# Ranking a gate's candidates by the softmax's sum, comparisons on ScalarE with TensorE counting, and one expert's activation placed earlier

## The chip, the cores and the metric

The kernel runs on one NeuronCore of a Trainium2 chip, in one launch. The metric is device microseconds of an execution, as the median of several runs. Five engines work side by side, each through its own list of instructions in order: TensorE (PE, its weight loads PEld), VectorE (DVE), ScalarE (ACT), GpSimd (POOL) and SyncE (SP), which here issues nearly all DMAs. SBUF and PSUM are the memories on the chip.

## The reference

The first half is a gated linear recurrence over 4 sequences of 5056 tokens with 256 channels; the second is a top-1 mixture of 8 experts with room for 80 tokens each.

```python
a_t = np.exp(8 * sigmoid(r_gate) * log_a_base)
x_gated = np.sqrt(np.maximum(1 - a_t * a_t, 1e-6)) * sigmoid(i_gate) * x
for t in range(S): h = a_t[:, t] * h + x_gated[:, t]; y[:, t] = h
# N = 20224 rows of y go to the experts
logits = x @ w_gate
expert_idx = np.argmax(logits, axis=1)
probs = np.exp(logits - logits.max(-1, keepdims=True))
probs /= probs.sum(-1, keepdims=True) + 1e-09
gate_w = probs[np.arange(N), expert_idx]
for e in range(8):
    # of the tokens whose argmax is e, the 80 with the largest gate_w
    h = np.maximum(x[tok_idx] @ w1[e], 0.0)
    out[tok_idx] = gate_w[tok_idx, None] * (h @ w2[e])
# every other row of out is zero
```

## The kernel before, in words

**Recurrence.** The tokens come in 40 blocks of 512 (`C`). A list written out by hand, `ORDER`, gives the order of all work of this half on every engine: loads, transposes on PE (L108, L142), tanh, exp and square root on ACT, products on POOL, the scan on DVE (L154). All states stay in SBUF, in the tile `Y`. Zeros go to the whole output from SP meanwhile (`zero_fill`, `wide_fill`).

**Gate.** PE forms logits from the states (L222). Six batches of blocks (`CHAINS`) go through eleven `stages`, which `ORDER` names c0.0 to c5.10: copy, transpose (L245), maximum, exp, the first expert at the maximum (`r_first`), the sum of the exps, then guard (L269), reciprocal (L271) and product (L274), a transpose back (`r_back`, L279) and a copy into `rows` (L283). After that each of 128 partitions of `rows` holds one expert's gate weights of a sixteenth of the tokens: partition 8j+e has expert e, share j. The token's weight stands in its own expert's row, zero in the other seven.

**Selection.** Written out in order in a block of its own, L391 to L451. Each partition takes its 14 largest weights (`K`): 8 with a maximum (L416), those replaced, the next 8 (L419). PE spreads the 14 of the 16 partitions that belong to one expert to all of them (L396), DVE scales them (`lowered`, L398). Then for each of the partition's own 14 a comparison with the expert's 224: `larger` compares on DVE (L401) and adds up on ACT (L402), for 12 of them (`SHARE`); `counted` does both on DVE (L404), for 2. The count is the candidate's rank. Between them stand, on POOL and DVE, the token numbers (L432 to L448) and the split of token and weight into parts in bf16 (`parts`, L410 to L413). PE runs twelve matmuls meanwhile whose result is not used (`keep_warm(WARM[0])`, L368), three before (`busy`, L101) and eight after. A comparison of the rank with 0 to 79 (L460) and 14 matmuls (L464) give each expert's 80 tokens and weights in order. A flag tells whether any partition had too few candidates; the arm for that does not run with these inputs.

**Experts.** Order by hand again (`experts`). For each expert the 80 tokens' columns are copied out of `Y`, split over ACT (`copies`, L544), POOL and DVE (L545) by the table `GATHER`, after each engine has loaded its token numbers into registers (`fetch`, L535). PE multiplies by w1 (`hidden`, L558), ACT applies the maximum with zero (`relu`, L563), PE multiplies by w2 (`summed`, L571), then a transpose (L586), the weight (`weigh`, L591) and a scatter into the output. Weights of two experts fit (`wbuf`): the loads of expert e+2 are issued from SP when `hidden(e)` and `summed(e)` are done with theirs (L322, L323), 512 KB each, four for an expert.

Of the kernel before, what the change touches and what calls it, by code (L numbers as in the profile page):

```python
# [19 lines left out]
SHARE = 12  # L20
WARM = (12, 8)
ZSLOT = 45
GATHER = ((28, 24), (28, 28), (32, 24))
# [36 lines left out]
def moe_kernel(ctx, tc, x, r_gate, i_gate, a_param, w_gate, w1, w2, out, capacity=80):  # L60
# [115 lines left out]
    nc.vector.tensor_tensor(fm, fm, bm, op=ALU.subtract)  # L176
# [12 lines left out]
    K1, NE = 16, P * EARLY  # L189
    rows = const.tile([P, NCOL + K1], F32, name="rows")  # L190
# [3 lines left out]
    for e in range(E): nc.gpsimd.memset(dio[:, e:e + 1], float(E - e))  # L194
# [102 lines left out]
    with tc.manual_schedule(engines={E_.Activation, E_.PE, E_.DVE, E_.Pool}):  # L297
        for task in ORDER.split():
            k, v = task[0], task[1:]
            if k in one_of: one_of[k](int(v))  # L300
            elif k in some_of: some_of[k](int(v.rstrip('+')), 1 + v.endswith('+'))
            elif k in half_of: half_of[k](int(v[:-1]), 'ab'.index(v[-1]))
            elif k == 'S': root(int(v.split(':')[0]), [int(m) for m in v.split(':')[1]])
            elif k == 'c': stages[int(v.split('.')[1])](int(v.split('.')[0]))
# [25 lines left out]
    V = 2 * E  # L330
    iot = lg[:, P:P + 80]
    se = lg[:, :P]
    nc.gpsimd.tensor_copy(se.rearrange("p (j e) -> p j e", e=E), em.unsqueeze(1).broadcast_to([P, NR, E]))
    nc.gpsimd.iota(iot, pattern=[[1, 80]], base=0, channel_multiplier=0, allow_small_or_imprecise_dtypes=True)
    small = lg[:, 208:512]
    comb = small[:, 210:210 + V]
# [45 lines left out]
    cmp = scr[:, 336:336 + 10 * 112].bitcast(BF16).rearrange("p (k j) -> p k j", k=10)  # L382
    oh = scr[:, 336:336 + K * CAP // 2].bitcast(BF16).rearrange("p (k s) -> p k s", s=CAP)
    vvf = scr[:, 1456:1712]; vv = vvf.rearrange("p (j k) -> p j k", j=NR)
    bd = scr[:, 1712:1968].rearrange("p (j k) -> p j k", j=NR)
    eq = scr[:, 1712:1968].rearrange("p (k q) -> p k q", k=16)
    late, tmp = rows[:, NE:], scr[:, 1200:1200 + K1 + NCOL - NE]
    pool, vec = nc.gpsimd, nc.vector
    pv = ps_t.tile([P, NR, 16], F32, name="pv")
    spare = bd  # L390
    with tc.manual_schedule(engines={E_.Activation, E_.PE, E_.DVE, E_.Pool}):  # L391
# [26 lines left out]
        vec.match_replace(tmp, cv[:, :8], late, -1.0)  # L418
        vec.max(cv[:, 8:], tmp)  # L419
        others_of(8, K)  # L420
        vec.max_index(ci[:, :8], cv[:, :8], late)
        lowered(0, 8); lowered(8, K)
        keep_warm(WARM[0], ps_t)
        parts(1, 3)
        larger(0)
        vec.max_index(ci[:, 8:], cv[:, 8:], tmp)
        pool.tensor_copy(pf, ci)
        larger(1)
# [3 lines left out]
        vec.tensor_tensor(eq, wide(pf), flat16(iot[:, :K1]), op=ALU.is_equal)  # L432
        pool.tensor_tensor(eq, eq, flat16(ecol), op=ALU.mult)
        larger(2); larger(3); larger(4)
        base(rk[:, :K], cv[:, :K], K)
        pool.tensor_scalar(lt, pf, float(K1), None, op0=ALU.is_ge)
        pool.tensor_scalar(cu.bitcast(F32), pf, float(NE - K1), None, op0=ALU.add)
        pool.tensor_tensor(lt, lt, cu.bitcast(F32), op=ALU.mult)
        vec.tensor_reduce(out=cf, in_=eq, op=ALU.add, axis=AX.X)
# [4 lines left out]
        for k in range(5, SHARE - 1): larger(k)  # L444
        vec.tensor_scalar(cu, cu, 5, None, op0=ALU.logical_shift_right)
        larger(SHARE - 1)
# [7 lines left out]
    nc.vector.tensor_scalar(fl, rk[:, K - 1:K], float(CAP), None, op0=ALU.is_lt)  # L454
# [12 lines left out]
    def general(K, ps):  # L467
# [9 lines left out]
        nc.vector.match_replace(rows[:, :NE], rows[:, NE + 8:NE + K1], rows[:, :NE], -1.0)  # L477
        bufs = (scr[:, :NCOL + K1], rows); cur = rows
        for r in range(K // 8):
# [3 lines left out]
            if r < K // 8 - 1:  # L483
                nc.vector.match_replace(bufs[r % 2], cv[:, sl], cur, -1.0)
# [12 lines left out]
        nc.vector.tensor_tensor(rk, rk, cnt, op=ALU.add)  # L497
# [13 lines left out]
    def experts(own, small_ps, ps, pool=True):  # L511
# [91 lines left out]
        def rows_of_slots():  # L603
# [5 lines left out]
            nc.vector.tensor_tensor(sidx, tk, none, op=ALU.add)  # L609
        small_ps.close()  # L610
# [75 lines left out]
```

## Time and profile before

| | us |
|---|---|
| median of 3 runs (294.41 to 295.31) | 294.52 |
| the profiled execution | 296.26 |
| its span, first to last instruction | 294.5 |
| busy: PE, DVE, ACT, POOL | 231.3, 212.6, 236.1, 209.4 |
| bytes moved by DMA, mean rate | 100.88 MB, 343 GB/s |

The span has three stretches: the recurrence up to about 214 us, the last gate batches and the selection up to 234, the experts up to the end. A time in the trace counts from the span's start. A row of the timeline has start, duration, engine, line, operation, tiles and shapes, a count where several were merged, and in brackets how long the engine had been idle and what ended that.

### The profile page before, as it was taken

The numbers are of one execution on the slowest core, as the hardware profiler recorded it, in microseconds if no ns is written. First come the engines' busy times: TensorE is split into PE (matmuls) and PEld (weight loads), VectorE is DVE, ScalarE is ACT, GpSimd is POOL, SyncE is SP. The second block draws the span as 40 slices with busy tenths as digits, with TensorE's granted clock in tenths as the row PEclk, the third lists the DMA queues.
The fourth block names the chain that finished last, engine by engine and source line by source line (L and its number), as shares of the span: only waits on it lengthen the run. The fifth ranks groups of instructions, "written<-read, shape, count | busy, mean of one in ns | idle before, by whom it ended". The sixth has DMA issues, their size and how long they took to land.

```text
span 294.5 us, 8439 instructions
## 1 busy us (share of the span) xinstructions
PE 231.3 (79%) x2816; PEld 189.6 (64%) x2816; DVE 212.6 (72%) x503; ACT 236.1 (80%) x480; POOL 209.4 (71%) x318
## 2 busy tenths in 40 slices
PE   2851796999988896897998888883786877999891
PEld 2750686777657764776765765852675667879780
DVE  2000596999989989999997999879968757566520
ACT  5899999999999999999999999599602457667600
POOL 2279999879959998998879964579204457775612
PEclk9965697999999999999999799799898999999997
DMA  6999799689999999999999999999999999999951
GB/s 216 417 410 410 273 415 411 240 320 416 410 406 337 347 375 352 359 365 325 374 352 368 333 340 323 335 312 325 406 395 409 355 379 343 328 358 356 319 159 31
DMA packets 42496, 100.88 MB, mean 343 GB/s; under 512 B 4048, under 2 KB 22352, under 8 KB 42448
## 3 DMA queue, kind: packets, MB, share of 16 engines
q1 hardware_dynamic: 42064, 99.64, 92.4%
q0 software_dynamic: 384, 0.66, 0.7%
q8 instruction: 24, 0.39, 0.5%
q14 instruction: 24, 0.20, 0.2%
HBM read 78.91 MB, written 21.36 MB: 341 GB/s over the span
## 4 chain that ended last, share of the span: by engine, by line
issue 11%; PE 11%; ACT 9%; DMA 9%; DVE 8%; POOL 6%; POOLq 2%; DVEq 1%; SPq 0%; ACTq 0%
DMA Y<-in_x_dram 5%; POOL Y L545 3%; ACT Y L119 3%; PE pd L368 2%; DVE Y L154 2%; DMA Y<-in_i_gate_dram 2%; PE pu L142 2%; ACT Y L131 2%; DMA Y<-in_moe_w_dram 2%; ACT Y L126 2%; POOLq L535 2%; ACT Y L110 2%; PE ph L558 2%; DVE pu L146 2%; PE pl L222 1%
## 5 line engine op out<-in xcount | busy, mean ns | idle before, releaser
L142 PE MATMUL pu<-ident,Y 128*128 128x128 f32 x632 | 91.5, 291 | 29.1 <-issue 10.4
L142 PEld LDWEIGHTS pu<-ident,Y 128*128 128x128 f32 x632 | 74.5, 149 | 48.4 <-issue 23.8
L154 DVE TENSOR_TENSOR_SCAN Y<-Y,pu 128x512 f32<-128x512 f32 (+4 forms) x86 | 100.6, 1179 | 2.7
L135 POOL TENSOR_TENSOR Y<-Y 128x1024 f32<-128x1024 f32 (+2 forms) x30 | 91.8, 3074 | 12.5 <-DMA Y<-in_x_dram 4.4
L122 POOL TENSOR_TENSOR Y<-Y 128x1024 f32<-128x1024 f32 (+2 forms) x30 | 72.8, 2438 | 24.1 <-ACT Y L119 11.8
L146 DVE SCALAR_TENSOR_TENSOR pu<-Y,pu 128x512 f32<-128x512 f32 (+1 forms) x80 | 53.6, 674 | 36.1 <-PE pu L142 32.5
L108 PE MATMUL pr<-ident,Y 128*128 128x128 f32 x316 | 46.6, 301 | 14.1 <-DMA Y<-in_r_gate_dram 8.1
L119 ACT ACTIVATE Y<-Y,tiny 128x512 f32<-128x512 f32 (+2 forms) x60 | 53.2, 945 | 0.3
L108 PEld LDWEIGHTS pr<-ident,Y 128*128 128x128 f32 x316 | 40.8, 157 | 16.6 <-ACT Y L110 10.2
L110 ACT ACTIVATE Y<-pr 128x1024 f32<-128x1024 f32 (+1 forms) x40 | 38.7, 1002 | 4.4 <-PE pr L108 4.4
L131 ACT ACTIVATE Y<-Y 128x1024 f32<-128x1024 f32 (+2 forms) x30 | 39.1, 1323 | 2.1 <-DMA Y<-in_i_gate_dram 1.5
L222 PE MATMUL pl<-Y 128*32 128x128 f32 (+2 forms) x704 | 40.4, 369 | 0.2 <-DVE Y L154 0.2
L126 ACT ACTIVATE Y<-Y 128x1024 f32<-128x1024 f32 (+2 forms) x30 | 37.9, 1319 | 0.1
L544 ACT COPY Y<-Y 128x2 f32 x248 | 24.7, 191 | 15.7 <-issue 10.6
L545 DVE COPY Y<-Y 128x2 f32 x196 | 22.3, 177 | 14.1 <-issue 14.1
L545 POOL COPY Y<-Y 128x2 f32 x196 | 24.8, 200 | 10.7 <-issue 10.7
L222 PEld LDWEIGHTS pl<-Y 128*32 128x32 f32 x704 | 19.9, 118 | 11.4 <-issue 5.0
L571 PE MATMUL po<-rows,Y 128*64 128x80 f32 x512 | 20.5, 235 | 3.8 <-ACT rows L563 2.2
L571 PEld LDWEIGHTS po<-rows,Y 128*64 128x64 f32 x512 | 18.7, 137 | 5.8 <-issue 2.7
L558 PE MATMUL ph<-Y 128*64 128x80 f32 x512 | 19.5, 234 | 2.9 <-DVE Y L545 2.1
L558 PEld LDWEIGHTS ph<-Y 128*64 128x64 f32 x512 | 18.5, 137 | 3.8 <-POOL Y L545 2.5
L126 ACT ACT_TABLE_LOAD x12 | 15.4, 1283 | 0.2
(137 smaller groups left out, 151.4 us busy)
## 6 DMA issues: line engine op xcount, KB each, us to landing
Y<-in_r_gate_dram SPq DMA_DIRECT2D x39, 512.0 KB, 7.2
Y<-in_i_gate_dram SPq DMA_DIRECT2D x39, 512.0 KB, 6.5
Y<-in_x_dram SPq DMA_DIRECT2D x39, 512.0 KB, 7.8
Y<-in_moe_w_dram SPq DMA_DIRECT2D x32, 512.0 KB, 6.0
out_dram<-Y SPq DMA_DIRECT2D x20, 512.0 KB, 6.7
out_dram<-Y SPq DMA_DIRECT2D x39, 256.0 KB, 7.0
Y<-in_r_gate_dram SPq DMA_DIRECT2D x1, 256.0 KB
Y<-in_i_gate_dram SPq DMA_DIRECT2D x1, 256.0 KB, 3.0
```

Source lines behind the costliest of these rows:

```text
L108: nc.tensor.transpose(pr[:, h, b:nb * P:nb], block('r', u, b, h), ident)
L110: nc.scalar.activation(rslot(u), prs.pop(u)[:, :, :ntok(u)], AF.Tanh, scale=0.5)
L119: nc.scalar.activation(a[:, :, h], z[:, :, h], AF.Exp, scale=L[:, h:h + 1], bias=L[:, h:h + 1])
L122: nc.gpsimd.tensor_tensor(pair('r', u, m), a, a, op=ALU.mult)
L126: nc.scalar.activation(q, q, AF.Sqrt, scale=-0.25, bias=0.25)
L131: nc.scalar.activation(i, i, AF.Tanh, scale=0.5)
L135: nc.gpsimd.tensor_tensor(i, i, v, op=ALU.mult)
L142: nc.tensor.matmul(pu[:, b:nb * P:nb], block(k, u, b, h), ident, is_transpose=True, start=(k == 'x' and b == 0), stop=(k == 'i' and b == n ...
L146: nc.vector.scalar_tensor_tensor(pu, rslot(u)[:, h], 0.5e-3, pu, op0=ALU.max, op1=ALU.mult)
L154: nc.vector.tensor_tensor_scan(y[:, s0:s1], a[:, s0:s1], q[:, s0:s1], init, op0=ALU.mult, op1=ALU.add)
L222: nc.tensor.matmul(pl[32 * j:32 * j + 32, c0:c0 + n], wg[:, h, 24 - E * k:WG - E * k], Y[:, us[0]:us[-1] + 1, h, 4 * j + k:ntok(us[0]):NR] ...
L545: else: eng.tensor_copy(dst, src)
```

## The change

**Value that is ranked.** The guard and the reciprocal of a batch go, and the product becomes a subtraction: in its own expert's row a token now holds minus the sum of its exps, in the others a number below -50. Weights 1/(sum + 1e-9) are formed for the chosen 80 at the end, two DVE instructions in `rows_of_slots`. Fill values become -1000.

**Comparisons.** Candidates are compared the other way round. Nine of the 14 on ACT: `Relu` with scale 2^40 and a bias for each partition, written as int8 into the low byte of bf16 numbers set to 128 before, so that a larger value adds 127. Five on DVE, written as bf16. The 14 results go to PE, which adds them over partitions and over candidates in one PSUM bank; DVE then keeps the partition's own part (a product, L470, and a sum, L471). No accumulator is read on ACT or DVE. Of the unused matmuls twelve become two; `busy` has four ahead of the transpose back and two more after each of the two spreads.

**Experts.** `relu(1)` moves ahead of ACT's last copies for expert 2, and `GATHER` gets an entry for each expert.

```diff
-SHARE = 12
-WARM = (12, 8)
+WARM = (2, 8)
-GATHER = ((28, 24), (28, 28), (32, 24))
+GATHER = ((28, 24), (28, 28), (28, 28), (28, 28), (28, 24), (32, 24), (28, 24), (32, 24))
...
-    nc.vector.tensor_tensor(fm, fm, bm, op=ALU.subtract)
+    nc.vector.scalar_tensor_tensor(fm, bm, 999.0, fm, op0=ALU.mult, op1=ALU.add)
...
-        d, key, top = view(pt, c), view(pt, c, 256), each(mx, c)
+        d, key, top = view(pt, c), view(lg, c, 256), each(mx, c)
         nc.vector.scalar_tensor_tensor(key, d, 0.0, dio[:d.shape[0]].unsqueeze(1).broadcast_to(list(d.shape)), op0=ALU.is_ge, op1=ALU.mult)
         nc.vector.tensor_reduce(out=top, in_=key, op=ALU.max, axis=AX.X)
-        nc.vector.tensor_tensor(view(lg, c, 256), key, spread(top), op=ALU.is_equal)
+        nc.vector.tensor_tensor(key, key, spread(top), op=ALU.subtract)
...
-    def r_guard(c):
-        by(c).tensor_scalar(each(sm, c), each(sm, c), 1e-9, None, op0=ALU.add)
-    def r_inverse(c):
-        nc.vector.reciprocal(each(sm, c), each(sm, c))
-    def r_weight(c):
+    def r_value(c):
         key = view(lg, c, 256)
-        by(c).tensor_tensor(key, key, spread(each(sm, c)), op=ALU.mult)
+        by(c).tensor_tensor(key, key, spread(each(sm, c)), op=ALU.subtract)
...
-        def larger(k):
-            c = cmp[:, k % 10]
-            vec.tensor_scalar(c.rearrange("p (j k) -> p j k", j=NR), vv[:, :, :K], cv[:, k:k + 1], None, op0=ALU.is_ge)
-            nc.scalar.activation(c, c, AF.Copy, accum_out=cnt[:, k:k + 1])
-        def counted(k):
-            vec.tensor_scalar(spare[:, :, :K], vv[:, :, :K], cv[:, k:k + 1], 0.0, op0=ALU.is_ge, op1=ALU.add, accum_out=cnt[:, k:k + 1])
+        def larger(q, k, act):
+            if act: nc.scalar.activation(low[q], vv[:, :, :K], AF.Relu, scale=BIG, bias=nb[:, k:k + 1])
+            else: vec.tensor_scalar(cmp[q].rearrange("p (j k) -> p j k", j=NR), vv[:, :, :K], cv[:, k:k + 1], None, op0=ALU.is_gt)
+        def summed(q, act, first, last):
+            nc.tensor.matmul(rps, seb[:, 0 if act else 1], cmp[q], start=first, stop=last)
+        nA = 9
+        def CA(k, first=False, last=False): larger(k % 4, k, True); summed(k % 4, True, first, last)
+        def CD(k): larger(4 + k % 3, nA + k, False); summed(4 + k % 3, False, False, False)
...
-        busy(3, ps_t.tile([P, 512], F32, name="pd"))
+        busy(4, bank)
...
+        vec.tensor_scalar(nb, cv, -BIG, None, op0=ALU.mult)
+        lowered(0, 8); lowered(8, K)
+        parts(1, 3)
+        CA(0, first=True); CA(1)
         vec.max_index(ci[:, :8], cv[:, :8], late)
-        lowered(0, 8); lowered(8, K)
-        keep_warm(WARM[0], ps_t)
...
         vec.tensor_scalar(cu, cu, 5, None, op0=ALU.logical_shift_right)
-        larger(SHARE - 1)
+        CA(8, last=True)
+        keep_warm(WARM[0], ps_t)
...
-        for k in range(SHARE, K): counted(k)
-        vec.tensor_tensor(rk[:, :K], rk[:, :K], cnt[:, :K], op=ALU.add)
+        vec.tensor_tensor(own[:, :, :K], rps.rearrange("p (j k) -> p j k", j=NR), bm.unsqueeze(2).broadcast_to([P, NR, K]), op=ALU.mult)
+        vec.tensor_reduce(out=red[:, :K], in_=own[:, :, :K].rearrange("p j k -> p k j"), op=ALU.add, axis=AX.X)
+        vec.tensor_tensor(rk[:, :K], rk[:, :K], red[:, :K], op=ALU.subtract)
...
-        for q in QS: first(q, 2); copies(q, 2)
+        for q in QS: first(q, 2)
+        copies('V', 2)
+        if pool: copies('P', 2)
+        copies('A', 2, 0, 20 if pool else 64)
         rows_of_slots()
         summed(0)
         hidden(1)
+        if pool: relu(1); copies('A', 2, 20)
         for k in range(1, E):
...
-            relu(k)
+            if k > 1 or not pool: relu(k)
```

On PE, from the warm-up ahead of the last transpose back (`pt`) to the flag's matmul (`pv` 1x1), before:

```order
L101 MATMUL pd<-ident 128x128 x3
L279 MATMUL pt<-ident,lg 128x112
L396 MATMUL pv<-Y,lg 128x16x8
L396 MATMUL pv<-Y,lg 128x16x6
L368 MATMUL pd<-Y,ident 128x256 x12
L456 MATMUL pv<-Y,lg 1x1
```

And the same place of the changed kernel; the pair at L412 is one comparison's weight load and matmul, and stands 14 times:

```order
L101 MATMUL pd<-ident 128x128 x4
L277 MATMUL pt<-ident,lg 128x112
L404 MATMUL pv<-Y,lg 128x16x8
L101 MATMUL pd<-ident 128x128 x2
L404 MATMUL pv<-Y,lg 128x16x6
L101 MATMUL pd<-ident 128x128 x2
L412 LDWEIGHTS Y
L412 MATMUL sel<-Y 128x224
...
L369 MATMUL pd<-Y,ident 128x256 x2
L477 MATMUL pv<-Y,lg 1x1
```

The transpose back now stands behind four unused matmuls, and fourteen counting matmuls have come in where ten unused ones went.

On DVE, the last part of the selection, from the sum that gives a token's column (`TENSOR_REDUCE` to `lg`) to the comparison with the 80 places, before:

```order
L439 TENSOR_REDUCE lg<-Y 128x16
L401 TENSOR_SCALAR Y<-Y,lg 128x224 x6
L445 TENSOR_SCALAR lg<-lg 128x16
L401 TENSOR_SCALAR Y<-Y,lg 128x224
L404 TENSOR_SCALAR Y,lg<-Y,lg 128x16x14 x2
L451 TENSOR_TENSOR lg<-lg 128x14
L454 TENSOR_SCALAR lg<-lg 128x1
L460 TENSOR_TENSOR Y<-lg 128x720
```

In the changed kernel:

```order
L458 TENSOR_REDUCE lg<-Y 128x16
L410 TENSOR_SCALAR Y<-Y,lg 128x224
L464 TENSOR_SCALAR lg<-lg 128x16
L470 TENSOR_TENSOR Y<-sel,Y 128x16x14
L471 TENSOR_REDUCE lg<-Y 128x14
L472 TENSOR_TENSOR lg<-lg 128x14
L475 TENSOR_SCALAR lg<-lg 128x1
L481 TENSOR_TENSOR Y<-lg 128x720
```

The shift of the token numbers (L445, now L464), for which POOL waits, has one comparison ahead of it instead of six, and two instructions on 224 numbers follow it.

On ACT, expert 1's activation (`rows<-ph`) among the copies for expert 2, from one load of token numbers to the next, before:

```order
L535 TENSOR_LOAD lg
L544 ISA
L544 COPY Y<-Y 128x2
...
L563 ACTIVATE rows<-ph 128x640
L581 COPY lg<-po 128x160
L535 TENSOR_LOAD lg
```

In the changed kernel, where the first stretch has 20 copies and the second 8:

```order
L556 TENSOR_LOAD lg
L565 ISA
L565 COPY Y<-Y 128x2
...
L584 ACTIVATE rows<-ph 128x640
L565 ISA
L565 COPY Y<-Y 128x2
...
L602 COPY lg<-po 128x160
L556 TENSOR_LOAD lg
```

The activation stood behind all 32 copies for expert 2 and now stands behind 20.

## Rows read from the trace of the kernel before

**Rows 1.** The page's DMA issues: tiles, engine, count, KB each, us to landing.

```profile
Y<-in_moe_w_dram SPq DMA_DIRECT2D x32, 512.0 KB, 6.0
```

**Rows 2.** Windows: us, busy of PE PEld DVE ACT POOL, granted PE clock, DMA share, GB/s.

```profile
226.00:228.00 2.00, 2.00 (x6) 1.64 (x5) 1.88 (x7) 1.35 (x7) 1.25 (x5) 0.50 1.00 395
...
246.00:249.00 3.00, 2.76 (x80) 2.60 (x76) 1.94 (x17) 1.94 (x20) 2.30 (x19) 1.00 0.95 309
...
252.00:255.00 3.00, 3.00 (x80) 2.72 (x78) 2.68 (x22) 2.56 (x28) 2.18 (x18) 1.00 0.84 283
...
270.00:280.00 10.00, 8.56 (x210) 7.69 (x211) 6.19 (x49) 6.92 (x61) 5.31 (x30) 1.00 0.94 317
```

**Rows 3.** Timeline, DVE and PE at the end of the last gate batch.

```profile
220.55 0.17 DVE L269 TENSOR_SCALAR Y<-Y 112x16 f32<-112x16 f32 x1
...
220.56 0.94 PE L101 MATMUL pd<-ident 128*128 128x128 f32 x6
...
220.76 0.25 DVE L271 RECIPROCAL Y<-Y 112x16 f32<-112x16 f32 x1
221.05 0.29 DVE L274 TENSOR_TENSOR lg<-lg,Y 112x128 f32<-112x128 f32 x1
...
221.40 0.32 PE L279 MATMUL pt<-ident,lg 112*128 112x112 f32 x1
```

**Rows 4.** Timeline, the selection from the scaled candidates to its last matmuls.

```profile
224.52 0.46 DVE L398 TENSOR_TENSOR Y<-pv,Y 128x128 f32<-128x128 f32 x2
...
225.12 7.11 PE L368 MATMUL pd<-Y,ident 128*128 128x256 f32 x24 [0.64 <-DVE Y L398]
...
228.46 1.59 DVE L401 TENSOR_SCALAR Y<-Y,lg 128x224 bf16<-128x224 f32 x6
...
230.30 0.28 POOL L447 TENSOR_SCALAR lg<-lg 128x16 f32<-128x16 int32 x1 [0.61 <-DVE lg L445]
...
230.78 0.45 DVE L404 TENSOR_SCALAR_CACHE_REDUCE Y<-Y,lg 128x224 f32<-128x224 f32 x1
...
231.22 0.38 POOL L411 TENSOR_TENSOR Y<-lg,Y 128x112 bf16<-128x112 bf16 x1
...
231.56 0.23 DVE L451 TENSOR_TENSOR lg<-lg 128x14 f32<-128x14 f32 x1 [0.33 <-ACT Y L402]
...
231.90 1.56 DVE L460 TENSOR_TENSOR Y<-lg 128x720 bf16<-128x720 f32 x2
...
232.11 0.92 POOL L411 TENSOR_TENSOR Y<-lg,Y 128x112 bf16<-128x112 bf16 x1
...
233.09 0.77 PE L464 MATMUL sel<-Y 128*48 128x80 bf16 x14 [0.74 <-POOL Y L411]
```

**Rows 5.** Lines of ACT, shapes apart: busy us, mean ns, idle before.

```profile
L119 ACT ACTIVATE Y<-Y,tiny 128x512 f32<-128x512 f32 x38 | 28.5, 809 | 0.1
...
L119 ACT ACTIVATE Y<-Y,tiny 128x1024 f32<-128x1024 f32 x20 | 23.7, 1238 | 0.2
...
L402 ACT ACTIVATE Y<-Y 128x224 bf16<-128x224 bf16 x12 | 4.5, 380 | 7.2 <-DVE Y L401 7.2
...
L402 ACT ACTIVATION_READ_ACCUMULATOR Y<-Y 128x1 f32 x12 | 2.2, 187 | 0.0
```

**Rows 6.** Timeline, PE and ACT from the start of the experts to expert 1's second product.

```profile
235.04 3.72 PE L368 MATMUL pd<-Y,ident 128*128 128x256 f32 x16
...
246.37 2.38 PE L558 MATMUL ph<-Y 128*64 128x80 f32 x64
...
246.94 3.35 ACT L544 COPY Y<-Y 128x2 f32 x32 [1.38 <-issue]
...
250.19 0.69 ACT L563 ACTIVATE rows<-ph 128x640 f32<-128x640 f32 x1
...
250.94 2.44 PE L571 MATMUL po<-rows,Y 128*64 128x80 f32 x64 [2.18 <-ACT rows L563]
```

**Rows 7.** Chain of waits, the piece behind expert 1's first product.

```profile
248.80 4.92 DMA Y<-in_moe_w_dram
```

More of the change, by code (lines that the diff above doesn't have):

```diff
@@ L9 @@
 I32 = mybir.dt.int32
+I8 = mybir.dt.int8
 U32 = mybir.dt.uint32
@@ L189, in moe_kernel @@
     K1, NE = 16, P * EARLY
+    LOW = -1000.0
     rows = const.tile([P, NCOL + K1], F32, name="rows")
@@ L193, in moe_kernel @@
     dio = tiny[:, 4:12]
-    for e in range(E): nc.gpsimd.memset(dio[:, e:e + 1], float(E - e))
+    for e in range(E): nc.gpsimd.memset(dio[:, e:e + 1], 100.0 * (E - e))
     lg = const.tile([P, C], F32, name="lg")
@@ L303, in moe_kernel @@
             elif k == 'S': root(int(v.split(':')[0]), [int(m) for m in v.split(':')[1]])
-            elif k == 'c': stages[int(v.split('.')[1])](int(v.split('.')[0]))
+            elif k == 'c':
+                if stages[int(v.split('.')[1])]: stages[int(v.split('.')[1])](int(v.split('.')[0]))
             elif k == 'Z': zero_fill(1)
@@ L330, in moe_kernel @@
     V = 2 * E
+    UNIT = 127
     iot = lg[:, P:P + 80]
@@ L333, in moe_kernel @@
     nc.gpsimd.tensor_copy(se.rearrange("p (j e) -> p j e", e=E), em.unsqueeze(1).broadcast_to([P, NR, E]))
-    nc.gpsimd.iota(iot, pattern=[[1, 80]], base=0, channel_multiplier=0, allow_small_or_imprecise_dtypes=True)
+    nc.gpsimd.iota(iot, pattern=[[UNIT, 80]], base=0, channel_multiplier=0, allow_small_or_imprecise_dtypes=True)
     small = lg[:, 208:512]
-    comb = small[:, 210:210 + V]
+    comb = small[:, 210:210 + V]; i16 = small[:, 226:242]
+    nc.gpsimd.iota(i16, pattern=[[1, K1]], base=0, channel_multiplier=0, allow_small_or_imprecise_dtypes=True)
     nc.vector.tensor_tensor(comb[:3 * V], ident[:3 * V, :V], ident[:3 * V, V:2 * V], op=ALU.add)
@@ L381, in moe_kernel @@
     rr = scr[:, :K * 3 * V // 2].bitcast(BF16).rearrange("p (k q v e) -> p k q v e", k=K, q=3, v=2)
-    cmp = scr[:, 336:336 + 10 * 112].bitcast(BF16).rearrange("p (k j) -> p k j", k=10)
+    KJ = NR * K
+    cmp = [scr[:, 336 + KJ // 2 * q:336 + KJ // 2 * (q + 1)].bitcast(BF16) for q in range(7)]
+    low = [scr[:, 336 + KJ // 2 * q:336 + KJ // 2 * (q + 1)].bitcast(I8).rearrange("p (j k b) -> p j k b", j=NR, b=2)[:, :, :, 0] for q in range(4)]
+    seb = scr[:, 1120:1248].bitcast(BF16).rearrange("p (q m) -> p q m", q=2)
     oh = scr[:, 336:336 + K * CAP // 2].bitcast(BF16).rearrange("p (k s) -> p k s", s=CAP)
[L384 to L387, printed above, removed]
+    tmp = scr[:, 1248:1248 + K1 + NCOL - NE]
+    vvf = scr[:, 1504:1760]; vv = vvf.rearrange("p (j k) -> p j k", j=NR)
+    bd = scr[:, 1760:2016].rearrange("p (j k) -> p j k", j=NR)
+    eq = scr[:, 1760:2016].rearrange("p (k q) -> p k q", k=16)
+    own = scr[:, 1760:2016].rearrange("p (j k) -> p j k", j=NR)
+    late = rows[:, NE:]
+    nb, red = small[:, 112:128], small[:, 242:258]
+    BIG = 2.0 ** 40
     pool, vec = nc.gpsimd, nc.vector
     pv = ps_t.tile([P, NR, 16], F32, name="pv")
-    spare = bd
+    rps = ps_t.tile([P, 512], F32, name="sel")[:, :KJ]
     with tc.manual_schedule(engines={E_.Activation, E_.PE, E_.DVE, E_.Pool}):
@@ L414, in moe_kernel @@
         pool.memset(rr[:, :, 2, 0], 0.0)
-        busy(3, ps_t.tile([P, 512], F32, name="pd"))
+        pool.tensor_copy(seb[:, 0], se)
+        pool.tensor_scalar(seb[:, 1], se, float(UNIT), None, op0=ALU.mult)
+        for q in range(4): pool.memset(cmp[q], 128.0)
+        bank = ps_t.tile([P, 512], F32, name="pd")
+        busy(4, bank)
         vec.max(cv[:, :8], late)
         others_of(0, 8)
-        vec.match_replace(tmp, cv[:, :8], late, -1.0)
+        busy(2, bank)
+        vec.match_replace(tmp, cv[:, :8], late, LOW)
         vec.max(cv[:, 8:], tmp)
         others_of(8, K)
+        busy(2, bank)
+        vec.tensor_scalar(nb, cv, -BIG, None, op0=ALU.mult)
+        lowered(0, 8); lowered(8, K)
+        parts(1, 3)
+        CA(0, first=True); CA(1)
         vec.max_index(ci[:, :8], cv[:, :8], late)
-        lowered(0, 8); lowered(8, K)
-        keep_warm(WARM[0], ps_t)
-        parts(1, 3)
-        larger(0)
         vec.max_index(ci[:, 8:], cv[:, 8:], tmp)
         pool.tensor_copy(pf, ci)
-        larger(1)
+        CA(2); CD(0); CA(3); CD(1)
         wide = lambda v: v.unsqueeze(2).broadcast_to([P, 16, K1])
         flat16 = lambda v: v.unsqueeze(1).broadcast_to([P, 16, K1])
[L432 to L435, printed above, removed]
+        vec.tensor_tensor(eq, wide(pf), flat16(i16), op=ALU.is_equal)
         pool.tensor_scalar(lt, pf, float(K1), None, op0=ALU.is_ge)
@@ L438, in moe_kernel @@
         pool.tensor_tensor(lt, lt, cu.bitcast(F32), op=ALU.mult)
+        pool.tensor_tensor(eq, eq, flat16(ecol), op=ALU.mult)
+        CA(4); CD(2)
+        base(rk[:, :K], cv[:, :K], K)
+        vec.tensor_scalar(rk[:, :K], rk[:, :K], float(UNIT * (KJ - K) + 128 * NR * nA), None, op0=ALU.add)
+        CA(5); CD(3); CA(6)
         vec.tensor_reduce(out=cf, in_=eq, op=ALU.add, axis=AX.X)
@@ L443, in moe_kernel @@
         pool.tensor_scalar(vals[:, 0], cf, float(NR), m1, op0=ALU.mult, op1=ALU.add)
-        for k in range(5, SHARE - 1): larger(k)
+        CA(7); CD(4)
         vec.tensor_scalar(cu, cu, 5, None, op0=ALU.logical_shift_right)
-        larger(SHARE - 1)
+        CA(8, last=True)
+        keep_warm(WARM[0], ps_t)
         pool.tensor_scalar(cf, cu, float(C), None, op0=ALU.mult)
@@ L476, in general @@
         eq = scr[:, :K * K1].rearrange("p (k q) -> p k q", q=K1)
-        nc.vector.match_replace(rows[:, :NE], rows[:, NE + 8:NE + K1], rows[:, :NE], -1.0)
+        nc.vector.match_replace(rows[:, :NE], rows[:, NE + 8:NE + K1], rows[:, :NE], LOW)
         bufs = (scr[:, :NCOL + K1], rows); cur = rows
@@ L483, in general @@
             if r < K // 8 - 1:
-                nc.vector.match_replace(bufs[r % 2], cv[:, sl], cur, -1.0)
+                nc.vector.match_replace(bufs[r % 2], cv[:, sl], cur, LOW)
                 cur = bufs[r % 2]
@@ L609, in rows_of_slots @@
             nc.vector.tensor_tensor(sidx, tk, none, op=ALU.add)
+            nc.vector.tensor_scalar(AT[:, E:], AT[:, E:], -1.0, 1e-9, op0=ALU.mult, op1=ALU.add)
+            nc.vector.reciprocal(AT[:, E:], AT[:, E:])
         small_ps.close()
```

14 lines of the change are left out of this document (7 added, 7 removed).

## The prediction

> **What bounds the kernel now.** I read the windows first, stretch by stretch, then the timeline from the last gate batch to the first experts, then the chain of waits, and the lines of ACT for the price of one comparison. The change touches nothing that the long recurrence waits for, so the last 75 us of the span count, and they have two parts.
>
> The first, from about 220 to 240 us, is one chain without slack: transpose back, candidates, comparisons, ranks, places, token numbers, gather. The reader sees in it that each step starts where another engine ends: POOL's token arithmetic waits 0.61 us for one shift on DVE, DVE's first use of the ranks waits 0.33 us for ACT, and the 14 matmuls that place the tokens wait 0.74 us for POOL's split of the token numbers [rows 4]. So at the end of the selection POOL is last, not ACT, although ACT's adding up is what the change replaces.
>
> The second, the experts, is held by PE and by the stream of weights together. There are 32 loads of 512 KB [rows 1], and the DMA share is 0.95 to 0.84 in two windows around expert 1 and 0.94 near the end [rows 2]; the rest of the time the engines are full. PE has one large hole: after expert 1's first product, which ends at 248.75 us, it waits 2.18 us for the activation, and ACT reaches this at 250.19 only, behind 32 copies for expert 2 [rows 6]. The chain of waits names a weight load there [rows 7].
>
> **The change part by part.** *Start of the selection.* Guard and reciprocal of the last batch go: from the start of L269 to the start of L274 DVE spends 0.50 us, so the value is ready at 220.84 instead of 221.34. But PE has four warm-up matmuls ahead of the transpose now. Six passes (three matmuls) took 0.94 us from 220.56, 0.157 each; eight take 1.25, and the transpose, which started 0.09 us ahead of the six passes' end, starts at 221.72 instead of 221.40 [rows 3]. The 0.50 us is lost and 0.3 us more: the selection starts 0.3 us late. If the passes follow each other closer, it is 0.1 us; below nothing it cannot be, since PE keeps its order. In the earlier batches the same instructions go from DVE at a time when the DMA engines are the limit; I count nothing, and nothing is lost if that cover goes.
>
> *DVE in the selection.* Twelve comparisons become five: seven at 1.59/6 = 0.265 us, 1.86 us. Two compare-and-count go, 0.48 us from one start to the next, 0.96 us. The wait for ACT, 0.33 us, goes [rows 4]. New are two small ones on 16 numbers (as L269, 0.17 us each [rows 3]) and two on 224 (as L404, 0.45 us each [rows 4]): 1.24 us. Net 1.9 us less; with the late start the ranks are ready 1.6 us sooner, at 230.2 instead of 231.79, if nobody makes DVE wait.
>
> *ACT in the selection.* Twelve ACTIVATEs of 0.380 us with twelve reads of 0.187 become nine ACTIVATEs. No row shows this form (f32 in, every second byte out, a bias by partition). From below, the same 224 numbers take 0.380 us [rows 5]. From above, L119 has scale and bias by partition: 0.809 us for 512 and 1.238 for 1024, so 0.84 ns a number and 0.38 us fixed, 0.57 us for 224 [rows 5]. Nine take 3.4 or 5.1 us; from 225.1 us they end at 228.5 or 230.2, the last counting matmul some 0.3 us later, and three DVE instructions (about 1.1 us) follow. At the lower end DVE is later anyway, at the upper one only 0.2 us of the selection is won. I take 0.40, nearest to the row with the same shape, and keep both ends.
>
> The Trainium skill, ScalarE: Activation LUTs, "What ACT_TABLE_LOAD costs", gives 186 ns and 0.833 ns an element for an ACTIVATE, 93 ns more for each per-partition operand, and 93 ns of overlap between two in a row; by it nine of these end after 3.45 us (an estimate), and the sum stays as it is. The trace agrees where it can: the formula gives 0.80 us for L119 on 512 numbers, the row has 0.809.
>
> *POOL.* The shift that it waits for stands behind one comparison instead of six; the 0.61 us goes. Its three small operations now run while DVE forms the 256-number comparison, ahead of the product instead of behind it, which is worth up to 0.5 us more. Against it, both numberings of candidates now end 0.2 us later than before, since they stand behind the scaling. Between 0.4 and 1.3 us sooner; I take 1.0. The last split took 0.92 us beside DVE's L460 where it took 0.38 without [rows 4]; it will meet that again, so nothing is won there. The placing matmuls start when POOL is done, at 232.1 instead of 233.09. **Selection: 1.0 us sooner**, range 0.2 to 1.5. The new casts and fills on POOL come while it waits for the last batch.
>
> *Experts.* Shifted by 1.0, ACT's copies for expert 2 start at 245.94. Twenty take 20 x 3.35/32 = 2.09 us, to 248.03, past the end of the product at 247.75; the activation's 0.69 us ends at 248.72, and the second product starts at about 248.8 instead of 250.94 [rows 6]: 2.1 us sooner, 1.1 of it from the move. The eight copies behind the activation and the fetch for expert 3 are late next: they push expert 3's gather, which limits what arrives to about 1.9 us. Four copies that ACT loses in three experts go to POOL or DVE, which have as many already; I count nothing, or 0.4 us either way if the balance shifts. The two new instructions for the weights stand where DVE waits for expert 2.
>
> The sum is 1.9 us. The profiled execution took 296.26 us, with a span of 294.5, so it would take 294.4; the median of the runs is 1.7 us below the profiled one, so the same difference gives 294.52 - 1.9 = **292.6 us**.
>
> **The rivals.** *The weights decide.* By the DMA shares the stream left about 3 x 0.05 + 3 x 0.16 = 0.6 us unused around expert 1 and 10 x 0.06 = 0.6 near the end [rows 2]. If loads of 512 KB that take 6.0 us to land [rows 1] cannot start earlier in step with PE, only part of the first 0.6 is gained: 0.4 us, 294.1 us. For it speaks the chain's DMA piece of 4.92 us [rows 7]; against it, that the second product of expert 1 was itself late and issues the loads of expert 3.
>
> *The selection gains nothing.* The late transpose, slow ACTIVATEs or POOL's split eat the 1.0; the move of the activation alone gives 1.1: 293.4 us. For it speak the upper price of ACT and the four warm-ups; against it, the three waits that vanish.
>
> *The clock.* Slower than before. PE stood mostly idle ahead of 225 us and was granted 0.50 in 226 to 228, the lower of 1.2 and 2.4 GHz [rows 2]; 24 passes took 7.11 us [rows 4], where 16 at the higher level took 3.72 [rows 6], so 24 would take 5.58: one drop cost 1.5 us of PE time. It was paid by matmuls that nobody waits for; ten of these twelve are gone, and the counting matmuls are short. One drop in the placing matmuls costs tenths. If two such drops reach the expert products, which have no slack, it is 3.0 us: 294.52 - 1.9 + 3.0 = 295.6 us. The second one decides. Against it stand the eight warm-ups ahead of expert 0, which remain.
>
> The Trainium skill, TensorE: Matmul & The Clock Gate, Part 1, says that the gate passes half the pulses by default and all of them when the array has been busy. By it this rival is open in principle; the row above agrees.
>
> **How the numbers follow.** Forecast 0.60 (291.3 to 293.5), selection without gain 0.15 (293.4), weights 0.15 (294.1), clock and other losses 0.10 (about 295.6). What this measurement can tell from no change is about 0.3%, 0.88 us: faster means under 293.6, slower over 295.4. The first two cases are faster, 0.75; the third is the same, 0.15; slower 0.10. The upper end of the range takes in the third case and half of the last, 295.2; the lower, 291.1, is a selection 1.5 us sooner and both 0.6 us of the stream filled with something to spare. Outside are about 0.06 on either side.
>
> **What would show it.** Transposing back at or after 221.6 us; nine ACTIVATEs within 3.4 to 4 us; the first DVE use of the counts without a wait for ACT; the placing matmuls at about 232, released by POOL; expert 1's second product within 0.2 us of the activation, near 248.8; the DMA share between 252 and 255 close to 1. I am wrong if ACT's comparisons last 5 us, if PE's clock is 0.50 in the first expert products, or if PE's holes behind expert 2 grow by what expert 1 saved.

## The result, and the profile after

The changed kernel takes 298.7 us (median of 4 runs, 297.9 to 300.3) against 294.47 of the kernel before (4 runs, 293.12 to 295.31): ratio 1.0147 [1.0102, 1.0191], **slower by about 4.3 us**. The prediction was 292.6, faster.

The profiled execution of before lay 1.8 us over its median, that of after 0.8 below its own, so the two traces differ by 1.4 us of span only (294.49 and 295.86). They still show the places. Against before, the last scan of the recurrence ends 2.04 us later (217.49, 215.45). From there to the placing matmuls it is 0.15 longer, from those to expert 1's second product 1.53 shorter, from that to expert 4's first product 3.25 longer, and from there to the end 2.54 shorter. The sum is 1.37. In that last stretch PE's products by w2 for experts 4 and 5 took 2.43 to 2.44 us, where before they took 2.76 to 2.81 and the one for expert 6 was broken by 1.20 us; that the loads of weights had run ahead during the longer wait is likely, but not shown.

**Recurrence.** First the view of one line, the third instruction of `r_first` (duration in ns: least, median, most), which had its `key` in PSUM before:

```profile
L264 DVE TENSOR_TENSOR lg<-pt,Y x6: 291/424/424, 84.5 to 220.0; 128x256 f32<-128x256 f32 x4, 128x128 f32<-128x128 f32 x1, 112x128 f32<-112x128 f32 x1
```

and after, where `key` stands in SBUF:

```profile
L265 DVE TENSOR_TENSOR lg<-lg,Y x6: 292/787/3267, 85.8 to 222.1; 128x256 f32<-128x256 f32 x4, 128x128 f32<-128x128 f32 x1, 112x128 f32<-112x128 f32 x1
```

The same instruction on the same 256 numbers now takes up to 3.27 us. The timeline of DVE and POOL around the longest one:

```profile
158.77 3.60 POOL L122 TENSOR_TENSOR Y<-Y 128x2048 f32<-128x2048 f32 x1
...
159.38 3.27 DVE L265 TENSOR_TENSOR lg<-lg,Y 128x256 f32<-128x256 f32 x1
...
162.33 4.71 POOL L135 TENSOR_TENSOR Y<-Y 128x2048 f32<-128x2048 f32 x1
162.57 0.68 DVE L146 SCALAR_TENSOR_TENSOR pu<-Y,pu 128x512 f32<-128x512 f32 x1
```

It started while a product of POOL ran, and ended 0.28 us after that product's end (162.37 to 162.65). The same batch of before, beside the same POOL product:

```profile
157.29 3.61 POOL L122 TENSOR_TENSOR Y<-Y 128x2048 f32<-128x2048 f32 x1
...
158.21 0.42 DVE L264 TENSOR_TENSOR lg<-pt,Y 128x256 f32<-128x256 f32 x1
160.55 1.29 DVE L146 SCALAR_TENSOR_TENSOR pu<-Y,pu 128x512 f32<-128x512 f32 x2 [1.91 <-ACT Y L126]
```

Here DVE is done in 0.42 us and then waits 1.91 for ACT: part of the 3.27 us falls into a wait that was there, the rest delays the scans. The Trainium skill, SBUF — State Buffer, "Who interferes with whom", states it as a rule: a DVE instruction with both inputs in SBUF contends with a GpSimd instruction that reads SBUF, and what they contend for, a shared pair of ports, is an exclusive lock. The trace agrees in three of six instances (1.15, 3.27 and 1.21 us); of the other three, two had no POOL product beside them, and one started 0.13 us before a product ended and took 0.42.

The 2.04 us by which the last scan ended later cannot be read as the price of this: in the traces with `key` in PSUM that scan ended anywhere from 213.72 (b3) to 216.99 us (c3).

**Selection.** The timeline that answers to [rows 3, 4]:

```profile
222.66 0.29 DVE L272 TENSOR_TENSOR lg<-lg,Y 112x128 f32<-112x128 f32 x1
...
223.03 1.16 PE L101 MATMUL pd<-ident 128*128 128x128 f32 x8
...
224.02 0.26 PE L277 MATMUL pt<-ident,lg 112*128 112x112 f32 x1
...
227.64 3.46 ACT L409 ACTIVATE Y<-Y,lg 128x224 int8<-128x224 f32 x9 [6.18 <-DVE Y L406]
...
229.99 0.80 DVE L410 TENSOR_SCALAR Y<-Y,lg 128x224 bf16<-128x224 f32 x1
230.00 0.65 POOL L453 TENSOR_TENSOR Y<-Y,tiny 128x256 f32<-128x256 f32 x1
...
231.73 0.17 DVE L464 TENSOR_SCALAR lg<-lg 128x16 int32<-128x16 int32 x1 [0.38 <-POOL lg L461]
...
232.80 0.21 DVE L472 TENSOR_TENSOR lg<-lg 128x14 f32<-128x14 f32 x1
...
233.12 1.58 DVE L481 TENSOR_TENSOR Y<-lg 128x720 bf16<-128x720 f32 x2
...
233.40 0.89 POOL L424 TENSOR_TENSOR lg<-lg 128x16 f32<-128x16 f32 x1
...
234.85 0.38 POOL L422 TENSOR_TENSOR Y<-lg,Y 128x112 bf16<-128x112 bf16 x1
...
235.28 0.68 PE L485 MATMUL sel<-Y 128*48 128x80 bf16 x14 [1.83 <-POOL Y L422]
```

The value is ready at 222.95 and its transpose starts at 224.02, behind the unused matmuls; before, the two stood 0.06 apart (221.34, 221.40). From the transpose on, the ranks (L472) come after 8.99 us where they came after 10.39, so DVE and ACT gave 1.4. The placing matmuls come after 11.26 us where it was 11.69: they wait 1.83 us for POOL's split, 0.74 before. DVE waits for POOL now (0.38), where POOL waited for DVE.

**Experts.** PE and POOL from expert 1's second product to expert 4's first one, in the timeline that answers to [rows 6]:

```profile
251.60 2.43 PE L592 MATMUL po<-rows,Y 128*64 128x80 f32 x64 [0.80 <-ACT rows L584]
...
257.76 2.44 PE L579 MATMUL ph<-Y 128*64 128x80 f32 x64 [1.02 <-POOL Y L566]
...
266.18 2.43 PE L579 MATMUL ph<-Y 128*64 128x80 f32 x64 [3.27 <-POOL Y L566]
```

and POOL's own rows:

```profile
253.93 3.67 POOL L566 COPY Y<-Y 128x2 f32 x28 [1.37 <-issue]
261.59 1.13 POOL L615 DMA_INDIRECT out_dram<-Y,lg  x1 [3.99 <-DMA Y<-in_moe_w_dram]
263.11 3.02 POOL L566 COPY Y<-Y 128x2 f32 x24 [0.39 <-issue]
```

The hole behind expert 1's first product has shrunk from 2.18 to 0.80 us. A new one of 3.27 has come ahead of expert 4's first product: the copies for expert 4 stand behind the first scatter in POOL's order, and POOL idles 3.99 us ahead of that scatter. The row that the scatter sends was ready at 256.41 and the copies ended at 257.60. The releaser named, a load of weights, is nothing that the scatter needs. Before, the scatter started at 254.83, 0.82 us behind the copies:

```profile
250.99 3.02 POOL L545 COPY Y<-Y 128x2 f32 x24 [1.24 <-issue]
254.83 1.14 POOL L594 DMA_INDIRECT out_dram<-Y,lg  x1 [0.82 <-DVE Y L545]
256.33 0.79 POOL L545 COPY Y<-Y 128x2 f32 x6 [0.37 <-issue]
257.30 2.27 POOL L545 COPY Y<-Y 128x2 f32 x18 [0.17 <-issue]
```

The last two rows are the copies for expert 4, which come behind that scatter; the break of 0.17 us between them is taken up below, under c3.

### The profile page after: what moved, and what is told of

The parts are those of the page before. It is cut to its first block, busy times and chain, and to the rows that moved or that the text cites. A ratio compares the mean times of both kernels' runs of the same rounds, so it can differ in the third digit from the quotient of the medians.

```text
span 295.9 us, 8429 instructions
## 1 busy us (share of the span) xinstructions
PE 226.3 (76%) x2820; PEld 184.9 (62%) x2820; DVE 214.6 (73%) x498; ACT 233.6 (79%) x449; POOL 212.0 (72%) x329
## 5 line engine op out<-in xcount | busy, mean ns | idle before, releaser
L108 PE MATMUL pr<-ident,Y 128*128 128x128 f32 x316 | 43.2, 284 | 17.0 <-DMA Y<-in_r_gate_dram 8.8
L108 PEld LDWEIGHTS pr<-ident,Y 128*128 128x128 f32 x316 | 36.8, 147 | 20.5 <-ACT Y L110 11.7
L565 ACT COPY Y<-Y 128x2 f32 x232 | 23.0, 191 | 15.8 <-issue 9.9
L566 POOL COPY Y<-Y 128x2 f32 x204 | 26.1, 199 | 10.9 <-issue 10.8
L566 DVE COPY Y<-Y 128x2 f32 x204 | 22.9, 175 | 14.2 <-issue 14.2
L592 PE MATMUL po<-rows,Y 128*64 128x80 f32 x512 | 19.5, 234 | 1.0 <-ACT rows L584 0.8
```

The lines of the kernel that those rows point to most:

```text
L108: nc.tensor.transpose(pr[:, h, b:nb * P:nb], block('r', u, b, h), ident)
L566: else: eng.tensor_copy(dst, src)
```

## The experiments

Two things were to be explained: DVE's long subtraction, and POOL's idle time at the first scatter. For the first the theory was the lock between DVE and POOL. For the second there were four: POOL has more copies (28 columns for experts 2 and 3, not 24); the scatter now stands at another place of POOL's program, eight copies further on; it waits for what the weights hold up in the DMA queues; or it is chance. Ratios are to runs of the kernel before that were taken together with these on the same chip; the medians of the three groups were 294.41, 295.2 and 296.0 us.

**a1_key_psum**: the changed kernel, `key` back in PSUM.

```diff
-        d, key, top = view(pt, c), view(lg, c, 256), each(mx, c)
+        d, key, top = view(pt, c), view(pt, c, 256), each(mx, c)
-        nc.vector.tensor_tensor(key, key, spread(top), op=ALU.subtract)
+        nc.vector.tensor_tensor(view(lg, c, 256), key, spread(top), op=ALU.subtract)
```

> The changed kernel with one thing undone: the key of the first expert is kept in PSUM again, so that the subtraction of its maximum (L265) has one operand in SBUF and not two. Theory 1 (DVE's subtraction with both operands in SBUF waits until a product that runs on POOL is over: 1.15, 3.27 and 1.21 us instead of 0.42 in the changed kernel's trace, and this is most of the loss): L265 takes 0.42 us or less everywhere, and the median falls by 2.5 to 4 us, from 298.7 to 294.7-296.2. Theory 2 (the loss sits in the experts, by the longer gather on POOL): the median stays at 297.5 or more. Theory 3 (the recurrence is only late by chance from run to run): L265 short, but the median within 0.9 us of 298.7.

297.68 us, 1.012 [1.0078, 1.0161]. The line's durations are those of before again:

```profile
L265 DVE TENSOR_TENSOR lg<-pt,Y x6: 291/424/424, 87.1 to 220.7; 128x256 f32<-128x256 f32 x4, 128x128 f32<-128x128 f32 x1, 112x128 f32<-112x128 f32 x1
```

The lock is shown by this; its price is the smaller part of the loss (0.27% of the time here, with intervals that overlap; the 2.5 to 4 us of the first theory did not come). POOL's idle time stayed: copies done at 255.71, first scatter at 261.47.

**a2_before_key_sbuf**: the kernel before with only that `key` in SBUF (`key = view(lg, c, 256)`).

> The kernel before with one thing of the change: the key of the first expert in SBUF, so that the comparison with its maximum (L264) has both operands in SBUF. Theory 1: that comparison takes more than 1 us in two or three of six batches, and the median rises from 294.5 by 2.5 to 4 us, to 297.0-298.5. Theories 2 and 3: 294.5, within 0.9 us.

296.98 us, 1.005 [1.0001, 1.0098]; the line takes up to 3.32 us. So the lock alone costs 0.3 to 0.5%, about 0.8 to 1.5 us, with this interval barely clear of nothing and those of a1 and the changed kernel overlapping, and again not the 2.5 to 4 us expected. The first scatter started at 258.31, 0.30 behind its row.

**a3_before_experts** and **a4_before_relu**: the kernel before with the activation moved, a3 with the new `GATHER`, a4 with the old one.

```diff
-        for q in QS: first(q, 2); copies(q, 2)
+        for q in QS: first(q, 2)
+        copies('V', 2)
+        if pool: copies('P', 2)
+        copies('A', 2, 0, 20 if pool else 64)
...
+        if pool: relu(1); copies('A', 2, 20)
```

> The kernel before with the expert part of the change alone: expert 1's activation ahead of ACT's last 12 (here 8 of 28) copies for expert 2, and the new table of shares. Theory 1: the expert part is a gain of about 1 us or nothing: 293.4 to 294.5. Theory 2: the 28 copies on POOL for experts 2 and 3 make its first scatter and the gather for expert 4 late, as in the changed kernel (PE waits 1.0 us for POOL ahead of expert 3 and 3.3 us ahead of expert 4): 295.5 or more.

> The kernel before with the earlier activation alone, shares as before (32, 24, 24 from expert 2 on; 12 copies of ACT come behind the activation). Expert 1's second product starts about 1.1 us sooner, at about 249.8 us of the trace. Theory 1: 293.4 to 294.2. Theory 2: as fast as that too, and 1 to 3 us faster than the run with the new shares; if the two are equal within 0.9 us, the shares cost nothing by themselves.

a3: 298.77 us, 1.0115 [1.0027, 1.0202]. a4: 293.41 us, 0.9941 [0.9898, 0.9983]. The move alone gains, the shares lose 1.7%, 5 us. POOL's rows in a3:

```profile
250.45 3.72 POOL L545 COPY Y<-Y 128x2 f32 x28 [1.38 <-issue]
259.26 1.14 POOL L594 DMA_INDIRECT out_dram<-Y,lg  x1 [5.09 <-DVE Y L545]
```

and in a4:

```profile
251.28 3.04 POOL L545 COPY Y<-Y 128x2 f32 x24 [1.17 <-issue]
255.32 1.14 POOL L594 DMA_INDIRECT out_dram<-Y,lg  x1 [1.00 <-DVE Y L545]
```

The four copies more take 0.68 us; the idle time behind them is 4.1 longer. The idle time thus has nothing to do with the selection. Chance is out too: of the 13 traces, the five in which the scatter stands further on in POOL's program have the idle time, and the eight others do not.

**b1_relu_pool_pad**: a4 with 16 more small fills on POOL ahead of the selection, where POOL waits; no copy moves between engines.

```diff
-        pool.memset(rr[:, :, 2, 0], 0.0)
+        for _ in range(17): pool.memset(rr[:, :, 2, 0], 0.0)
```

> The kernel before with the earlier activation and the old shares, and 16 more memsets of the same cells on POOL in its idle time before the selection; they do no work that is used. With them POOL's first scatter stands as many instructions into POOL's program as it does with the new shares (16 more). With the new shares POOL stood still for 3.7 to 5 us ahead of that scatter, with DVE's row long ready. Theory 4 (place: POOL waits for its own next instructions there, behind the weights in the DMA queues; it depends on where in the program the scatter stands): the stall of 3 to 5 us comes back, PE waits 3 to 5 us for POOL ahead of expert 4, and the median is 296 to 298.5. Theory 5 (shares: 28 copies on POOL for experts 2 and 3 make the scatter wait): no stall, 293.0 to 294.0.

296.23 us, 1.0025 [0.9984, 1.0067], where a4 had 0.9941: 0.8%, 2.5 us, for the place alone. The fills ran from 212.8 to 217.1 us; the idle time is back, 40 us later:

```profile
250.94 3.04 POOL L545 COPY Y<-Y 128x2 f32 x24 [1.20 <-issue]
258.67 1.14 POOL L594 DMA_INDIRECT out_dram<-Y,lg  x1 [4.69 <-issue]
```

**b3_newshares_place_kept**: a4 with the new shares but for the first two entries, so that POOL copies 100 columns ahead of the first scatter (20, 24, 28, 28), as many as before (24, 28, 24, 24), and not 108.

```diff
-GATHER = ((28, 24), (28, 28), (32, 24))
+GATHER = ((28, 20), (28, 24), (28, 28), (28, 28), (28, 24), (32, 24), (28, 24), (32, 24))
```

> The kernel before with the earlier activation and the new shares, except that POOL has 4 copies fewer for experts 0 and 1 each (DVE has them), so that its first scatter stands at the same place of its program as before, although it has 28 copies for experts 2 and 3. Theory 4 (place): no stall ahead of the first scatter, median 293 to 294.8. Theory 5 (shares): a stall of 3 to 5 us as in the run with the new shares alone, 297 to 299.

294.93 us, 0.9993 [0.9951, 1.0035].

```profile
248.94 3.62 POOL L545 COPY Y<-Y 128x2 f32 x28 [1.45 <-issue]
254.23 1.14 POOL L594 DMA_INDIRECT out_dram<-Y,lg  x1 [1.67 <-DVE Y L591]
```

28 copies as in a3, and the scatter starts where its row is ready (L591). So it is the place in POOL's program, not the number of copies for an expert: b1 moves the place and leaves the copies, b3 the other way round. Against a3 the old place saves 1.2%; against a4 these shares still cost 0.5%, with intervals that overlap.

**c3_no_loads_expert3**: a3 without the loads for expert 3.

```diff
-                if e + 2 < E: load_w1(e + 2, h)
+                if e + 2 < E and e != 1: load_w1(e + 2, h)
```

(and the same for `load_w2`).

> The kernel before with the activation moved and the new shares, which had the wait ahead of the first scatter (259.26 us, copies done at 254.16), and here without the four weight loads of expert 3 (2 MB); expert 3 then multiplies by the weights of expert 1. Theory (POOL waits there for its own instructions, which come behind weights in the DMA queues): the first scatter starts within 1.5 us of POOL's last copy, near 254.5 to 255.5 us; the fetch of 8 KB that lay ahead of the release lands early. Rival (the wait belongs to the place in the program alone, whatever the DMA queues hold): again 4 to 5 us behind the copies. The time itself says little, since 2 MB of 100.88 MB are missing (6 us at 343 GB/s).

298.27 us, 1.0129 [1.0076, 1.0182], with 2 MB less to move.

```profile
254.12 3.71 POOL L545 COPY Y<-Y 128x2 f32 x28 [1.30 <-issue]
261.47 1.14 POOL L594 DMA_INDIRECT out_dram<-Y,lg  x1 [3.64 <-DVE Y L545]
```

A window just ahead of it (length, busy time of PE, PEld, DVE, ACT and POOL, granted clock, DMA share, GB/s) shows the DMA engines nearly empty:

```profile
254.00:256.50 2.50, 2.50 (x68) 2.22 (x63) 2.04 (x18) 2.29 (x25) 2.38 (x19) 1.00 0.04 9
```

In the idle time itself they were not:

```profile
257.83:261.47 3.64, 3.59 (x90) 3.31 (x92) 1.91 (x14) 2.36 (x22) 0.00 (x1) 1.00 0.85 335
```

The expectation of the theory, 1.5 us, is missed: 3.64 us remain. But the run does not rule a backlog out, since from 256.22 us on SP issued the next loads of weights, which kept the DMA engines busy while POOL waited (0.85). Nor does it show that one costs anything: 3.64 lies close to the 3.99 us of the changed kernel, which has all its loads. How much a backlog adds is open. The view of the DMA queues has two transfers of 8 KB of instructions in the window from 258 to 260 us, after the copies' end at 257.83:

```profile
q14 instruction: 2, 0.02, 2.6%
```

In every run with the idle time such a transfer lies within 2.5 us ahead of the release, but transfers of this kind lie there in runs without it too. That POOL waits for its own instructions would fit the place's effect.

Something else in the traces speaks for it. Number all of POOL's records in the trace from 0, register and semaphore instructions too, which the timeline leaves out, in the order of the program. In every one of the 13 runs there is a step of about 0.4 us between records, in place of about 0.1, at record 452, and again at 324 and 580, 128 records to either side. Where the scatter stands at the old place, record 452 lies behind it, among the copies for expert 4, and costs a break of 0.17 us in before. In the five runs with the idle time it lies two records ahead of the scatter (a3, b1, c3) or five (after, a1). So the first scatter idles where it comes just behind a spot at which POOL's program halts in any case. That this spot is where POOL takes in new instructions is a guess: no row names what POOL waits for, and it stays open.

**b2_after_psum_oldshares**: the changed kernel with both undone, `key` in PSUM and the old `GATHER`.

> The changed kernel with the key in PSUM again and the old shares (28,24), (28,28), (32,24); what stays is the ranking by the sum, the comparisons on ACT with PE's counting, and the earlier activation. Theory 1 with theory 4 or 5 (the key's place and the shares are the whole loss): no subtraction over 0.45 us, no stall at the first scatter, 292.3 to 293.5, that is 0.9 to 2 us under the kernel before. If the selection itself costs time: above 294.5.

295.39 us, 0.995 [0.9892, 1.0009]; the first scatter at 253.74, 0.79 behind the copies. Of the whole change the two causes take 2%. Against a4 (0.9941) it also says what selection and ranked value are worth together: nothing that these intervals, 0.4 to 0.6% to either side, can tell from zero.

**b4_b2_one_warmup**: b2 with `busy(1, bank)` in place of `busy(4, bank)` ahead of the transpose.

> As the changed kernel with the key in PSUM and the old shares, and with one unused matmul instead of four ahead of the last transpose back. If the transpose waits for these matmuls (it started 1.07 us after DVE had its input in the changed kernel): it starts within 0.15 us of DVE's end, the selection is 0.7 to 1.0 us sooner, and the median 0.3 to 1.0 us under that run. Rival: the clock falls to the lower level in the selection and takes it back, no difference within 0.5 us.

294.72 us, 0.9922 [0.9884, 0.996]: faster than before, and the lowest ratio of all, though its interval overlaps those of b2 and a4.

```profile
219.55 0.29 DVE L272 TENSOR_TENSOR lg<-lg,Y 112x128 f32<-112x128 f32 x1
...
220.10 0.49 PE L101 MATMUL pd<-ident 128*128 128x128 f32 x2
...
220.43 0.26 PE L277 MATMUL pt<-ident,lg 112*128 112x112 f32 x1
```

The transpose starts 0.59 us behind the value, not 1.07; the 0.15 expected was missed, with an unused matmul still ahead of it.

**c1_after_place_kept** and **c2_best_new_shares**: the changed kernel, and b4, both with the shares of b3.

> The changed kernel with one edit: the first two entries of the new shares are (28, 20) and (28, 24), so that POOL copies 100 columns ahead of the first scatter, as before the change, and not 108; the gate's key stays in SBUF. Theory (two causes, the place of the first scatter in POOL's program and the subtraction that waits for POOL's products): no wait of some 4 us ahead of the first scatter, which starts within 1.3 us of POOL's last copy; the last scan still near 217.5 us, so a span of 292.5 to 294.5, and 1.5 to 4 us less than the changed kernel, about level with the kernel before. Rival (POOL's wait comes with the changed selection or with DMA traffic that only happened to fall so): the first scatter again 3 us or more behind POOL's copies, 297 to 299 us.

> The best version so far (the changed kernel, key in PSUM, shares of before, one unused matmul ahead of the transpose back) with the new shares, their first two entries (28, 20) and (28, 24). If the new shares are worth something once the place is kept: 0.3 to 1 us below that version, ratio to before 0.988 to 0.991. If they are worth nothing or cost something, as their run without the changed selection says (0.9993 against 0.9941 of the run with the shares of before): 0.994 to 1.000.

c1: 297.11 us, 1.0089 [1.0043, 1.0134]; no idle time ahead of the first scatter (256.55, its row ready at 256.24), and 0.6% less than the changed kernel, at the low end of what was expected, with intervals that overlap; it did not come level with the kernel before. c2: 295.52 us, 1.0028 [0.9987, 1.007]: the shares cost b4 about 1% even at the old place. DVE's and PE's rows of c1 at expert 3:

```profile
254.40 1.43 DVE L566 COPY Y<-Y 128x2 f32 x12 [1.59 <-issue]
...
256.69 0.99 DVE L566 COPY Y<-Y 128x2 f32 x8 [0.16 <-issue]
...
257.98 2.43 PE L579 MATMUL ph<-Y 128*64 128x80 f32 x64 [2.06 <-issue]
```

and of b4:

```profile
251.36 1.46 DVE L566 COPY Y<-Y 128x2 f32 x12 [1.60 <-issue]
...
255.06 2.44 PE L579 MATMUL ph<-Y 128*64 128x80 f32 x64 [1.04 <-ACT Y L565]
```

PE waits 2.06 us in place of 1.04. In b4 ACT with its 32 copies is last; in c1 it is DVE (to 257.68), which has four columns more in each of experts 0 and 1 by these shares, starts its copies for expert 3 later against PE (0.91 us behind the start of the product for expert 2, in b4 0.23 ahead of it), and ends last. By these rows c1 and c2 pay for the old place with DVE's time; what the shares would be worth without either was not tried.

## Why the prediction was wrong, point by point

**The step that failed: "Four copies that ACT loses in three experts go to POOL or DVE ... I count nothing, or 0.4 us either way."** They cost 1.7% of the time, 5 us (a3 less a4; a1 less b2 gives the same). The balance of the engines was looked at, if with three experts where the table has four (2, 3, 4 and 6), and shows as 0.7 us of copies on POOL. What was not looked at: the shares also move the first scatter along POOL's program, and at the new place POOL idles some 4 us. The place is worth 0.8% (b1 less a4) to 1.2% (a3 less b3), 2.5 to 3.6 us. The rest goes with the shares at the old place too, 0.5% in b3 and 1.1% in c2, where DVE has the copies that POOL was spared. One sign of being wrong that the prediction named came true: PE's hole ahead of expert 4 grew from 0.72 to 3.27 us, more than the 1.38 that expert 1 had saved. No row of before could have priced this, and the range should have been wider for an edit that lengthens an engine's program ahead of a step that others wait for.

**"In the earlier batches the same instructions go ... I count nothing."** The step counted what goes and overlooked that the remaining subtraction gets both operands from SBUF while POOL multiplies: 0.8 to 1.5 us (a1, a2). This could have been read: the diff shows `key` moving, and the POOL products beside this instruction in the trace of before last 1.25 to 3.60 us.

**The selection, 1.0 us sooner.** Nothing that can be told from zero (b2 against a4), the rival "the selection gains nothing". ACT was right: nine ACTIVATEs took 3.46 us, 0.384 each, next to the lower end of 0.380 (0.40 was taken); the Trainium skill, ScalarE: Activation LUTs, "What ACT_TABLE_LOAD costs", gave 3.45 as an estimate. So were DVE's wait for ACT, which went, and the late transpose: 0.88 us behind the value by the working, 1.07 measured. Wrong was POOL's "1.0 sooner". Its end came 0.4 sooner, counted from the transpose, where the working, with a transpose 0.3 late, needed 1.3; one DVE comparison beside its product was stretched from 0.32 to 0.80, and its subtraction L424 beside L481 from 0.22 to 0.89. Three warm-ups less may give back 0.3% (b4 against b2, whose intervals overlap).

**The move of the activation, 1.1 us.** Right: the second product of expert 1 comes 0.80 us behind the first, 1.5 sooner counted from the placing matmuls, and alone the move gives 0.6%, 1.7 us (a4), with an interval (0.2 to 1.0%) that holds the 1.1.

**The other rivals.** The weights did not decide: the DMA share was high, but PE's new hole ends with POOL's copies. The clock did not either: it was granted 0.50 in 238 to 240 us and 1.00 in every window from 242 us to the last products. The sum of the terms as measured, each from its own pair of runs, is +5.1 (shares and place), +0.8 to 1.5 (`key`), about 0 (selection), -1.7 (activation): 4.2 to 4.9, against 4.3 measured.

## What to carry to other kernels

Ask of every edit what it does to the operands' memories and to the instructions behind it, not only how many instructions come and go: an operand moved from PSUM to SBUF can make a short DVE instruction as long as the POOL product beside it. Count copies into an engine's program as a shift of everything after them, and after the run compare the idle time ahead of its first DMA with that of before. Where a change has independent parts, time them apart: here one part gained 1.7 us, two lost 6, and the version with the lowest ratio (b4) keeps the gain.

## What the runs showed of the hardware

- A DVE subtraction of 256 numbers took 0.42 us with one operand in PSUM and up to 3.27 or 3.32 with both in SBUF, ending 0.28 us after the POOL product that ran when it started (after and a2, twice each).
- POOL idled 3.6 to 5.8 us ahead of its first scatter in the runs where that stood 8 copies or 16 small fills further on in its program (after, a1, a3, b1, c3), and started it 0.8 to 1.0 us behind its copies, or 0.3 us after the scatter's row was ready, where it stood at the old place (before, a2, a4, b2, b3, b4, c1, c2). Leaving out 2 MB of loads left 3.64 us of it, with the DMA engines busy again meanwhile.
- POOL's records in the trace stand about 0.4 us apart at numbers 324, 452 and 580 in all 13 runs, where those around them stand about 0.1 apart; the long wait came only where the scatter stood two or five records behind the second of these spots.
- The profile named three different releasers for the same wait (a load of weights in the changed kernel, a DVE copy in a1, a3 and c3, "issue" in b1): there the name is no evidence, the length and place of the idle time are.
